# Two transformer layers with sliding-window attention on one core: priorities for evictions and masks, MLP values in half buffers, score maxima cut at PSUM banks

## The chip, the cores and the metric

One Trainium2 chip, one of its cores. The metric is the device time of one execution in microseconds. Engines are named as in the profile: PE (TensorE, its matmuls; PEld its weight loads), DVE (VectorE), ACT (ScalarE), POOL (GpSimd), SP (SyncE, which issues most transfers).

## What is computed

Two layers, each an attention block and an MLP block over 2048 tokens of width 640, with the same weights in both layers:

```python
H = 32; Dh = D // H; W = 256              # D = 640, F = 1536
qkv = (layernorm(x) @ wqkv).reshape(B, S, 3, H, Dh)
scores = einsum("bhqd,bhkd->bhqk", q, k) * Dh ** -0.5
mask = (i - j >= 0) & (i - j < W)          # i: query, j: key
p = softmax(where(mask, scores, -1e9))
x = x + einsum("bhqk,bhkd->bhqd", p, v).reshape(B, S, D) @ wo
h = layernorm(x) @ w1 + b1
x = x + (relu(h) ** 2) @ w2 + b2           # and the same again for layer 2
```

All is float32 outside. Inside, the kernel carries each operand of the projections as two float16 parts, a high one and the rest, and multiplies high by high, high by low and low by high (`mm3`, three matmuls for each step of the contraction).

## The kernel before

**Units and quads.** The tokens go in groups of T = 256. A unit `u` is one group in one layer: 8 groups by 2 layers, 16 units. The 32 heads of a unit go in 8 quads of four heads. For each quad there are three pieces of attention work:

- `max_quad`: the scores with queries on the partitions (L300, a block of 16 matmuls into the two PSUM tiles `bb` of three banks each), then on DVE, for each of four pieces (two head pairs `j`, two query blocks `i`) and two halves `e` of the partitions, an in-place add of the mask with a maximum along the row (L308, eight reduces, each followed by a read of its accumulator). A piece has 384 columns; the four lie one behind the other in the 1536 columns of a tile, so the second crosses from bank 0 to bank 1 and the third from bank 1 to bank 2. The reduces are traced after all 16 matmuls.
- `exp_quad`: the scores again, transposed, keys on the partitions, with the row maxima taken away through two extra rows of the contraction (L344, 16 matmuls into the same two `bb` tiles, one bank for each of three steps), then six exponentials on ACT (L353, each 128x512 into a tile `pt`) and the triangular masks on POOL (L362, L366, eight for a quad).
- `pv_quad`: 32 matmuls of probabilities by values into `pv` (L391), then the copy `po` out of PSUM on ACT (L401), transposes and a reciprocal on DVE (L404 to L407), the product on POOL (L408), and the split into two float16 parts `ot` (L411 on ACT, L412 on DVE). `max_out` transposes the maxima of four quads (L316), splits them into `mT` on DVE (L318, L319) and sends them into rows of `qt`.

**Dense stages.** While unit `u` does its attention, PE also does, in pieces between the quads, `stage_qk` and `stage_v` of unit `u + 1`, `stage_o` and the MLP `stage_f` of unit `u - 1`. Each accumulates in a PSUM tile `acc`, which is evicted: `qd` (L237 on ACT, then L238 on DVE), `vt` (L264 on ACT), `x1` (L442 and L491 on DVE), and in the first half of `stage_f`, for two of the 12 blocks of F at a time, two relus into one buffer `r` of 128x512 (L476, ACT), its square on POOL (L478), the high part on ACT (L479) and the rest on DVE (L480) into `hh`. The second half multiplies `hh` by w2. The tag `mm` has two PSUM buffers of one bank, shared by `acc`, `tr` and `pv`; the two `bb` tiles take the other six banks and are shared in turn by `exp_quad` and `max_quad`.

**What sets the order.** PE's order is the order in which the program traces its instructions (`manual_schedule`). `together` writes it: for each quad the exponentials' matmuls, then dense work, then the maxima's matmuls of a quad five ahead and pv, then dense work again; `SHARE` is the part of a quad's dense work that stands between the exponentials' matmuls and pv. The orders of ACT, DVE, POOL and SP are made before the run by a planner that walks through estimated times: whenever an engine is free in its plan, it takes of the instructions whose inputs are ready the one with the lowest priority number, by default the one traced first. `tc.high_priority(offset=400)` gives the instructions traced inside it a number lower by 400. On the chip an engine then keeps the order planned. Waits are put in by the framework from the tiles that the instructions read and write.

Of the kernel before, what the change touches and what calls it, by code (L numbers as in the profile page):

```python
# [42 lines left out]
def kernel(ctx: ExitStack, tc: tile.TileContext, x, wqkv, wo, w1, b1, w2, b2, out):  # L43
# [120 lines left out]
    def split_t(y, dst):  # L164

        for c0, n in ((0, 3), (3, 2)):
            tr = ps.tile([P, 4, P], F32, name="tr", tag="mm", bufs=2)
            for c in range(n):
                nc.tensor.transpose(tr[:, c, :], y[:, (c0 + c) * P:(c0 + c + 1) * P], ident)
            nc.scalar.copy(dst[:, 0, c0:c0 + n], tr[:, :n])  # L170
            nc.vector.tensor_sub(dst[:, 1, c0:c0 + n], tr[:, :n], dst[:, 0, c0:c0 + n])  # L171
            yield 117 * n

    xs = [tc.dram_tile([P, D], F32, name=f"xs{i}") for i in range(S // P)]
# [47 lines left out]
    def stage_qk(u, hold=False):  # L222
        yT = yTs[u]
        qt = sb.tile([P, NP, T], F16, name="qt", tag="qt", bufs=2)
        kt = kts[u % 3]
        qts[u] = qt
        for j, dst in enumerate((qt, kt)):
            qd = sb.tile([P, KC, 2, T], F16, name="qd", tag="qd", bufs=1)
            for c0 in range(0, KC, 2):
                n = min(2, KC - c0)  # L230
                acc = ps.tile([P, 2, T], F32, name="acc", tag="mm", bufs=2)
                for c in range(n):
                    lo = j * D + (c0 + c) * P
# [3 lines left out]
                at[0] = nc.scalar.activation(qd[:, c0:c0 + n, 0, :], acc[:, :n, :], AF.Copy, scale=s)  # L237
                nc.vector.scalar_tensor_tensor(qd[:, c0:c0 + n, 1, :], acc[:, :n, :], s, qd[:, c0:c0 + n, 0, :],  # L238
                                               op0=ALU.mult, op1=ALU.subtract)
# [16 lines left out]
    def stage_v(u):  # L256
        yT = yTs.pop(u)
        for i in range(2):
            vt = vts[(2 * u + i) % 6][0]
            for h in range(2):  # L260
                acc = ps.tile([P, 2, T], F32, name="acc", tag="mm", bufs=2).rearrange("p a n -> p (a n)")
                yield from mm3(acc[:, :HD], lambda a, k: yT[:, a, k, i * P:(i + 1) * P],
                               lambda b, k: wq_s[:, b, k, 2 * D + h * HD:2 * D + (h + 1) * HD], KC, 136)
                at[0] = nc.scalar.activation(vt[:, h * NP:(h + 1) * NP, 0:DH],  # L264
                                             acc[:, :HD].rearrange("p (h d) -> p h d", d=DH),
                                             AF.Copy, scale=1.0 / (YS * WS))


    GQ = NQ // 2
# [5 lines left out]
    def max_quad(n):  # L275

        u, qd = divmod(n, NQ)
        g = u % NG
        qt, cur, prev = qts[u], kts[u % 3], kts[(u - 1) % 3]
        G = qd // GQ  # L280
        if (u, G) not in mxs:
            mxs[u, G] = sb.tile([P, 2, 2, 2 * GQ], F32, name="mx", bufs=2)
        mx = mxs[u, G]
        bb = [b.rearrange("p a n -> p (a n)") for b in banks()]
        found = []
        for j in range(2):
            p = 2 * qd + j
            for i in range(2):
                parts = [(prev, 0, T, 0), (cur, 0, P, T)] if i == 0 else [(prev, P, T, 0), (cur, 0, T, P)]
                if g == 0:  # L290
                    parts = parts[1:]
                o = parts[0][3]
                base = 3 * P * (2 * j + i)
                for kt, a, b, c in parts:
                    while a < b:

                        z = min(b, a + 512 - (base + c) % 512)
                        for e in range(2):
                            r = slice(64 * e, 64 * e + 3 * DH)
                            nc.tensor.matmul(bb[e][:, base + c:base + c + z - a], qt[r, p, i * P:(i + 1) * P],  # L300
                                             kt[r, p, a:z], start=True, stop=True)
                        a, c = z, c + z - a
                for e in range(2):
                    s0 = p % (2 * GQ)
                    found.append((bb[e][:, base + o:base + 3 * P], maskb[:, o:], mx[:, i, e, s0:s0 + 1]))

        for w, mask, to in found:
            nc.vector.tensor_tensor_reduce(out=w, in0=w, in1=mask, scale=1.0, scalar=-3.0e38,  # L308
                                           op0=ALU.add, op1=ALU.max, accum_out=to)

    def max_out(u, G):

# [5 lines left out]
        nc.vector.tensor_scalar(mT[:, 0], tr[:NR, 0, :], -1.0 / MS, None, op0=ALU.mult)  # L318
        nc.vector.scalar_tensor_tensor(mT[:, 1], tr[:NR, 0, :], -1.0 / MS, mT[:, 0],  # L319
                                       op0=ALU.mult, op1=ALU.subtract)  # L320
        for i in range(2):
            for e in range(2):
                s0 = (2 * i + e) * 2 * GQ
# [7 lines left out]
    def exp_quad(n):  # L331
# [2 lines left out]
        qt = qts[u]  # L334
        bb = banks()
        steps = steps_of(u)
        for k, step in enumerate(steps):
            o = 0
            for kb, kt, ko, q0, qn in step:
                w = qn * P  # L340
                for j in range(2):
# [2 lines left out]
                        nc.tensor.matmul(bb[e][:, k, o:o + w], kt[r, 2 * qd + j, ko:ko + P],  # L344
                                         qt[r, 2 * qd + j, q0 * P:q0 * P + w], start=True, stop=True)
                    o += w
        out = []
        for k, step in enumerate(steps):
            pts = []
            for e in range(2):  # L350
                o = sum(2 * qn * P for _, _, _, _, qn in step)
# [3 lines left out]
                for kb, kt, ko, q0, qn in step:  # L355
                    w = qn * P
                    pj = pt[:, o2:o2 + 2 * w].rearrange("p (j n) -> p j n", j=2)
                    o2 += 2 * w
                    if kb < 2:

                        m = pj[:, :, w - P:w]
                        nc.gpsimd.affine_select(out=m, in_=m, pattern=[[0, 2], [-1, P]],  # L362
                                                compare_op=ALU.is_gt, fill=0.0, base=0, channel_multiplier=1)
                    else:
                        m = pj[:, :, 0:P]
                        nc.gpsimd.affine_select(out=m, in_=m, pattern=[[0, 2], [1, P]],  # L366
                                                compare_op=ALU.is_ge, fill=0.0, base=0, channel_multiplier=-1)
                    pts.append((e, kb, q0, qn, pj))
            out.append(pts)
        return out  # L370
# [8 lines left out]
    def pv_quad(n, quad):  # L379
# [21 lines left out]
        nc.scalar.copy(po, pv)  # L401
# [33 lines left out]
    def stage_o(u):  # L435
        for i in range(2):
            od, x1 = ols.pop((u, i))
            for h in range(2):
                acc = ps.tile([P, 2, T], F32, name="acc", tag="mm", bufs=2).rearrange("p a n -> p (a n)")
                hs = slice(h * HD, (h + 1) * HD)  # L440
                yield from mm3(acc[:, :HD], lambda a, k: od[:, k, a, :], lambda c, k: wo_s[:, c, k, hs], KC, 136)
                nc.vector.scalar_tensor_tensor(x1[:, hs], acc[:, :HD], 1.0 / (OS * WS), x1[:, hs],  # L442
                                               op0=ALU.mult, op1=ALU.add)
# [19 lines left out]
    def stage_f(u, ahead=None):  # L463
# [3 lines left out]
        hh = sb.tile([P, 2, FC, T], F16, name="hh", tag="hh", bufs=1)  # L467
        for f0 in range(0, FC, 2):
            acc = ps.tile([P, 2, T], F32, name="acc", tag="mm", bufs=2)
            r = sb.tile([P, 2, T], F32, name="r", bufs=1)  # L470
            for f in range(2):
                fo = (f0 + f) * P
                yield from mm3(acc[:, f, :], lambda a, k: w1_s[:, a, k, fo:fo + P],
                               lambda c, k: y2[:, c, k, :], KC, 109)
            for f in range(2):
                nc.scalar.activation(r[:, f, :], acc[:, f, :], AF.Relu, bias=b1s[:, f0 + f:f0 + f + 1],  # L476
                                     scale=1.0 / (YS * WS))
            nc.gpsimd.tensor_tensor(r, r, r, op=ALU.mult)  # L478
            nc.scalar.copy(hh[:, 0, f0:f0 + 2, :], r)  # L479
            nc.vector.tensor_sub(hh[:, 1, f0:f0 + 2, :], r, hh[:, 0, f0:f0 + 2, :])  # L480
        if ahead is not None:
            ln_cross(ahead)
        for i in range(2):
            b = 2 * g + i
            x1 = x1s.pop((u, i))
            for h in range(2):
# [4 lines left out]
                nc.vector.scalar_tensor_tensor(x1[:, hs], acc[:, :HD], 1.0 / WS, x1[:, hs],  # L491
                                               op0=ALU.mult, op1=ALU.add)
            dst = xs[b] if l + 1 < NL else out_rows[b * P:(b + 1) * P, :]
            nc.sync.dma_start(dst, x1)

# [6 lines left out]
        for _ in chain(*gs):  # L502
            pass

    SHARE = 0.5
    LEAD = GQ + 1
    late = []

# [139 lines left out]
```

## Time and profile before

| | |
|---|---|
| median of 3 runs | 1810.35 us (1807.04 to 1821.32) |
| the profiled execution's own time | 1810.7 us |
| its span, first to last instruction | 1809.0 us |
| mean granted TensorE clock | 0.974 |
| PE busy | 1625.9 us, 90% of the span |
| DVE busy | 1068.8 us, 59% |
| ACT busy | 765.0 us, 42% |
| POOL busy | 715.0 us, 40% |

How to read the lines that follow. A row of the waits has the engine, the tile and line of the waiting instruction, an arrow, what released it, and then the total in us, how often, and the longest. A row of the timeline has start and length in us, the engine, the line, the operation, out<-in, and the number of instructions that were merged into it; brackets at the end hold the idle time ahead of it and what ended that. A row of the table of stretches has the stretch, its length, the busy time of PE, PEld, DVE, ACT and POOL with the number of instructions, then the granted clock, the busy share of the transfer engines and the GB/s. A row of the groups has the shape, the count, the busy time in us, the mean of one in ns, and the idle time ahead with its releasers. Overlapping matmuls make a "busy" PE a little less than a full one.

### The profile page before, as it was taken

The numbers are of one execution on the slowest core, as the hardware profiler recorded it, in microseconds if no ns is written. First come the engines' busy times: TensorE is split into PE (matmuls) and PEld (weight loads), VectorE is DVE, ScalarE is ACT, GpSimd is POOL, SyncE is SP. The second block draws the span as 40 slices with busy tenths as digits, with TensorE's granted clock in tenths as the row PEclk, the third lists the DMA queues.
The fourth block names the chain that finished last, engine by engine and source line by source line (L and its number), as shares of the span: only waits on it lengthen the run. The fifth ranks groups of instructions, "written<-read, shape, count | busy, mean of one in ns | idle before, by whom it ended". The sixth has DMA issues, their size and how long they took to land.

```text
span 1809.0 us, 44389 instructions
## 1 busy us (share of the span) xinstructions
PE 1625.9 (90%) x17286; PEld 1179.0 (65%) x17286; DVE 1068.8 (59%) x3377; ACT 765.0 (42%) x1620; POOL 715.0 (40%) x1338
## 2 busy tenths in 40 slices
PE   5767698999999989999899999999999999997798
PEld 4544476676666767666677767667676666764567
DVE  6546465757666565766556666666656666655331
ACT  5464243443444344444434343444434344442422
POOL 4353343434334343433425253433525344342422
PEclk9889899999999999999999999999999999998899
DMA  6754104235151423515153422515243251511010
GB/s 198 186 162 108 42 25 120 47 89 111 35 143 42 125 56 88 111 35 143 42 134 63 121 64 77 124 34 140 45 116 66 71 129 34 139 17 56 16 37 30
DMA packets 239059, 154.81 MB, mean 86 GB/s; under 512 B 80640, under 2 KB 219776, under 8 KB 238848
## 3 DMA queue, kind: packets, MB, share of 16 engines
q1 hardware_dynamic: 230432, 142.46, 32.0%
q10 hardware_dynamic: 8416, 9.51, 1.8%
q8 instruction: 136, 2.23, 0.5%
q14 instruction: 75, 0.61, 0.1%
HBM read 82.58 MB, written 52.43 MB: 75 GB/s over the span
## 4 chain that ended last, share of the span: by engine, by line
PE 55%; DVE 20%; ACT 8%; DMA 7%; POOL 4%; issue 3%; SPq 2%; ACTq 0%; POOLq 0%; DVEq 0%
PE acc L145 42%; DVE bb L308 11%; PE pv L391 5%; ACT pt L353 5%; PE bb L300 4%; PE bb L344 4%; DVE mx L308 2%; POOL po L408 1%; DMA qk<-qd 1%; DVE bst L157 1%; SPq L326 1%; ACT r L476 1%; DMA xt<-in_A_x_dram 1%; DMA stg<-in_B_w_dram 1%; POOL pt L366 1%
## 5 line engine op out<-in xcount | busy, mean ns | idle before, releaser
L308 DVE CUSTOM_DVE_ANT_0 bb<-bb,maskb 128x384 f32<-128x384 f32 (+2 forms) x1024 | 511.2, 559 | 154.3 <-PE bb L300 154.1
L353 ACT ACTIVATE pt<-bb 128x512 f32<-128x512 f32 x736 | 368.7, 601 | 86.7 <-PE bb L344 86.4
L408 POOL TENSOR_TENSOR po<-po,rb 128x256 f32<-128x256 f32 x128 | 94.6, 739 | 675.5 <-DVE rb L407 580.4
L145 PE MATMUL acc<-y,w_s 128*128 128x256 f16 x2880 | 335.4, 275 | 3.5 <-DVE y L171 1.5
L145 PE MATMUL acc<-w_s,hh 128*128 128x320 f16 x2304 | 326.3, 299 | 0.4 <-DVE hh L480 0.2
L145 PEld LDWEIGHTS <-w_s 128*128 128x128 f16 x2880 | 278.5, 99 | 62.9 <-issue 27.5
L145 PE MATMUL acc<-yT,wq_s 128*128 128x256 f16 x2400 | 290.0, 281 | 12.0 <-DVE qd L238 7.1
L145 PEld LDWEIGHTS <-hh 128*128 128x128 f16 x2304 | 221.7, 98 | 98.4 <-issue 14.5
L145 PEld LDWEIGHTS <-wq_s 128*128 128x128 f16 x2400 | 235.5, 100 | 66.2 <-issue 33.0
L391 PE MATMUL pv<-pt,vt 128*32 128x128 f32 (+1 forms) x3840 | 202.2, 341 | 61.3 <-ACT r L476 31.8
L362 POOL TENSOR_SCALAR_AFFINE_SELECT pt<-pt 128x256 f32<-128x256 f32 x448 | 192.4, 434 | 147.5 <-ACT pt L353 134.1
L366 POOL TENSOR_SCALAR_AFFINE_SELECT pt<-pt 128x256 f32<-128x256 f32 x512 | 201.2, 416 | 9.8 <-ACT pt L353 8.9
L401 ACT COPY po<-pv 128x256 f32<-128x256 f32 x128 | 47.5, 371 | 342.7 <-PE pv L391 342.7
L391 PEld LDWEIGHTS pv<-pt,vt 128*32 128x32 f32 x3840 | 110.7, 112 | 115.6 <-issue 50.9
L145 PE MATMUL acc<-wo_s,od 128*128 128x320 f16 x960 | 143.3, 305 | 30.5 <-DMA od<-o 17.7
L145 PE MATMUL acc<-wq_s,yT 128*128 128x320 f16 x960 | 144.5, 299 | 12.8 <-DVE mT L319 7.9
L478 POOL TENSOR_TENSOR r<-r 128x512 f32<-128x512 f32 x96 | 99.9, 1041 | 116.7 <-ACT r L476 112.5
L145 PEld LDWEIGHTS <-od 128*128 128x128 f16 x960 | 92.4, 99 | 79.0 <-issue 25.4
L308 DVE DVE_READ_ACCUMULATOR2_ANT mx<- 128x1 f32 x1024 | 142.5, 139 | 0.0
L411 ACT CAST ot<-po 128x256 f16<-128x256 f32 x128 | 52.1, 407 | 195.7 <-POOL po L408 195.6
L145 PEld LDWEIGHTS <-yT 128*128 128x128 f16 x960 | 92.3, 98 | 59.6 <-issue 25.5
L238 DVE SCALAR_TENSOR_TENSOR qd<-acc,qd 128x512 f16<-128x512 f32 (+1 forms) x96 | 55.4, 578 | 126.4 <-ACT qd L237 126.4
(62 smaller groups left out, 1427.0 us busy)
## 6 DMA issues: line engine op xcount, KB each, us to landing
qk<-qd SPq DMA_DIRECT2D x32, 640.0 KB
qt<-qk SPq DMA_DIRECT2D x32, 480.0 KB
kt<-qk SPq DMA_DIRECT2D x32, 480.0 KB
qk<-qd SPq DMA_DIRECT2D x32, 320.0 KB
o<-ot SPq DMA_DIRECT2D x256, 40.0 KB
od<-o SPq DMA_DIRECT2D x32, 320.0 KB
stg<-in_B_w_dram ACTq DMA_DIRECT2D x30, 256.0 KB
xt<-in_A_x_dram SPq DMA_DIRECT2D x16, 320.0 KB
```

Source lines behind the costliest of these rows:

```text
L145: nc.tensor.matmul(acc, lhs(a, c), rhs(b, c), start=(k == 0), stop=(k == 3 * nk - 1))
L238: nc.vector.scalar_tensor_tensor(qd[:, c0:c0 + n, 1, :], acc[:, :n, :], s, qd[:, c0:c0 + n, 0, :], op0=ALU.mult, op1=ALU.subtract)
L300: nc.tensor.matmul(bb[e][:, base + c:base + c + z - a], qt[r, p, i * P:(i + 1) * P], kt[r, p, a:z], start=True, stop=True)
L308: nc.vector.tensor_tensor_reduce(out=w, in0=w, in1=mask, scale=1.0, scalar=-3.0e38, op0=ALU.add, op1=ALU.max, accum_out=to)
L344: nc.tensor.matmul(bb[e][:, k, o:o + w], kt[r, 2 * qd + j, ko:ko + P], qt[r, 2 * qd + j, q0 * P:q0 * P + w], start=True, stop=True)
L353: at[0] = nc.scalar.activation(pt[:, :o], bb[e][:, k, :o], AF.Exp, scale=SCALE / (QS * QS))
L362: nc.gpsimd.affine_select(out=m, in_=m, pattern=[[0, 2], [-1, P]], compare_op=ALU.is_gt, fill=0.0, base=0, channel_multiplier=1)
L366: nc.gpsimd.affine_select(out=m, in_=m, pattern=[[0, 2], [1, P]], compare_op=ALU.is_ge, fill=0.0, base=0, channel_multiplier=-1)
L391: nc.tensor.matmul(pv[32 * jj:32 * (jj + 1), q0 * P:(q0 + qn) * P], vf[:, c:c + 32], pj[:, j, :], start=(k == 0), stop=(k == len(steps) - ...
L408: nc.gpsimd.tensor_tensor(po, po, rb.rearrange("p a b -> p (a b)"), op=ALU.mult)
L411: nc.scalar.copy(oh, pf)
L478: nc.gpsimd.tensor_tensor(r, r, r, op=ALU.mult)
```

## The change

It has five parts.

1. A helper `first()` (priority 400 places ahead) is put around the instructions that empty the `mm` buffers in PSUM (`split_t`, `qd`, `vt`, `mT`, `po`, both `x1` updates, the relus) and around the masks on POOL.
2. In `stage_f` the buffer `r` of 128x512 becomes two buffers of 128x256, one for each block of F, and square, high part and rest are done for each by itself: 96 more of each.
3. In `max_quad` three pieces have a bank each (columns 0 to 383), and the fourth is spread over the last 128 columns of the three banks. Its matmuls come first, cut into 128 columns; its reduces come last and read three banks. The reduces of each other piece are traced behind that piece's matmuls. A quad has 18 matmuls for the maxima in place of 16 (10 in place of 8 in the first unit of a layer).
4. In `exp_quad` the exponentials and masks of a step are traced behind that step's matmuls, and no longer behind those of all three.
5. `SHARE` goes from 0.5 to 0.55.

```diff
+    def first():
+        return tc.high_priority(offset=400)
...
+                with first():
+                    at[0] = nc.scalar.activation(qd[:, c0:c0 + n, 0, :], acc[:, :n, :], AF.Copy, scale=s)
+                    nc.vector.scalar_tensor_tensor(qd[:, c0:c0 + n, 1, :], acc[:, :n, :], s, qd[:, c0:c0 + n, 0, :],
+                                                   op0=ALU.mult, op1=ALU.subtract)
...
-        bb = [b.rearrange("p a n -> p (a n)") for b in banks()]
+        bb = banks()
         found = []
-        for j in range(2):
+        for w in (3, 0, 1, 2):
+            j, i = divmod(w, 2)
             p = 2 * qd + j
...
+            if w == 3:
+                parts = [(kt, z, z + P, c + z - a) for kt, a, b, c in parts for z in range(a, b, P)]
+            for kt, a, b, c in parts:
                 for e in range(2):
+                    r = slice(64 * e, 64 * e + 3 * DH)
+                    to = bb[e][:, c // P, 3 * P:] if w == 3 else bb[e][:, w, c:c + b - a]
+                    nc.tensor.matmul(to, qt[r, p, i * P:(i + 1) * P], kt[r, p, a:b], start=True, stop=True)
+            now = []
+            for e in range(2):
...
+                if w == 3:
+                    now.append((bb[e][:, o // P:, 3 * P:], maskb[:, o:].rearrange("p (a n) -> p a n", n=P), accum))
+                else:
+                    now.append((bb[e][:, w, o:3 * P], maskb[:, o:], accum))
+            if w == 3:
+                found = now
+                continue
+            for v, mask, accum in now + (found if w == 2 else []):
+                nc.vector.tensor_tensor_reduce(out=v, in0=v, in1=mask, scale=1.0, scalar=-3.0e38,
+                                               op0=ALU.add, op1=ALU.max, accum_out=accum)
...
+        out = []
         for k, step in enumerate(steps):
...
                         nc.tensor.matmul(bb[e][:, k, o:o + w], kt[r, 2 * qd + j, ko:ko + P],
                                          qt[r, 2 * qd + j, q0 * P:q0 * P + w], start=True, stop=True)
                     o += w
-        out = []
-        for k, step in enumerate(steps):
             pts = []
...
-            r = sb.tile([P, 2, T], F32, name="r", bufs=1)
...
-            for f in range(2):
-                nc.scalar.activation(r[:, f, :], acc[:, f, :], AF.Relu, bias=b1s[:, f0 + f:f0 + f + 1],
-                                     scale=1.0 / (YS * WS))
-            nc.gpsimd.tensor_tensor(r, r, r, op=ALU.mult)
-            nc.scalar.copy(hh[:, 0, f0:f0 + 2, :], r)
-            nc.vector.tensor_sub(hh[:, 1, f0:f0 + 2, :], r, hh[:, 0, f0:f0 + 2, :])
+            rs = [sb.tile([P, T], F32, name="r", bufs=2) for f in range(2)]
+            with first():
+                for f, r in enumerate(rs):
+                    nc.scalar.activation(r, acc[:, f, :], AF.Relu, bias=b1s[:, f0 + f:f0 + f + 1],
+                                         scale=1.0 / (YS * WS))
+            for f, r in enumerate(rs):
+                nc.gpsimd.tensor_tensor(r, r, r, op=ALU.mult)
+                nc.scalar.copy(hh[:, 0, f0 + f, :], r)
+                nc.vector.tensor_sub(hh[:, 1, f0 + f, :], r, hh[:, 0, f0 + f, :])
...
-    SHARE = 0.5
+    SHARE = 0.55
```

More of the change, by code (lines that the diff above doesn't have):

```diff
@@ L317, in max_out @@
         mT = sb.tile([NR, 2, P], F16, name="mT", bufs=1)
[L318 to L320 removed]
+        with first():
+            nc.vector.tensor_scalar(mT[:, 0], tr[:NR, 0, :], -1.0 / MS, None, op0=ALU.mult)
+            nc.vector.scalar_tensor_tensor(mT[:, 1], tr[:NR, 0, :], -1.0 / MS, mT[:, 0],
+                                           op0=ALU.mult, op1=ALU.subtract)
         for i in range(2):
@@ L400, in pv_quad @@
         po = sb.tile([P, T], F32, name="po", bufs=2)
-        nc.scalar.copy(po, pv)
+        with first():
+            nc.scalar.copy(po, pv)
         rb = sb.tile([P, T // 32, 32], F32, name="rb", bufs=1)
@@ L441, in stage_o @@
                 yield from mm3(acc[:, :HD], lambda a, k: od[:, k, a, :], lambda c, k: wo_s[:, c, k, hs], KC, 136)
-                nc.vector.scalar_tensor_tensor(x1[:, hs], acc[:, :HD], 1.0 / (OS * WS), x1[:, hs],
-                                               op0=ALU.mult, op1=ALU.add)
+                with first():
+                    nc.vector.scalar_tensor_tensor(x1[:, hs], acc[:, :HD], 1.0 / (OS * WS), x1[:, hs],
+                                                   op0=ALU.mult, op1=ALU.add)
             y = sb.tile([P, D], F32, name="xt", tag="xt", bufs=2)
@@ L490, in stage_f @@
                                lambda c, k: w2_s[:, c, k, hs], FC, 136)
-                nc.vector.scalar_tensor_tensor(x1[:, hs], acc[:, :HD], 1.0 / WS, x1[:, hs],
-                                               op0=ALU.mult, op1=ALU.add)
+                with first():
+                    nc.vector.scalar_tensor_tensor(x1[:, hs], acc[:, :HD], 1.0 / WS, x1[:, hs],
+                                                   op0=ALU.mult, op1=ALU.add)
             dst = xs[b] if l + 1 < NL else out_rows[b * P:(b + 1) * P, :]
```

57 lines of the change are left out of this document (22 added, 35 removed).

## The prediction

> **What bounds the kernel now.** I read the engine shares first, then the table of stretches, the waits of PE, and the timeline of one unit (the attention of 256 tokens and the dense stages beside it).
>
> ```profile
> span 1809.0 us, 44389 instructions
> PE 1625.9 (90%) x17286; PEld 1179.0 (65%) x17286; DVE 1068.8 (59%) x3377; ACT 765.0 (42%) x1620; POOL 715.0 (40%) x1338
> ...
> 496.50:602.50 106.00, 99.41 (x1115) 72.91 (x1110) 67.55 (x209) 45.89 (x97) 42.79 (x84) 1.00 0.34 86
> ```
>
> PE is busy for 90% of the span; no other engine is near its limit. The last row is one unit: 106.00 us, PE busy 99.41, granted clock 1.00, then DVE 67.55, ACT 45.89, POOL 42.79. So a unit has 6.6 us of idle PE, and that is all that an edit of the order can win there. The waits say what it is. PE's waits in the even part, 390 to 1541 us (1151 us, or 10.9 units; total, times, longest):
>
> ```profile
> PE pv L391 <- ACT r L476: 26.6, 12, 3.1
> PE pv L391 <- POOL pt L366: 15.8, 20, 1.5
> PE acc L145 <- DVE qd L238: 13.2, 20, 1.0
> PE acc L145 <- DVE mT L319: 6.6, 10, 0.7
> PE acc L145 <- ACT vt L264: 2.3, 10, 0.3
> ...
> PE bb L344 <- DVE mx L308: 0.2, 1, 0.2
> ```
>
> The same kinds over the whole run:
>
> ```profile
> PE pv L391 <- ACT r L476: 31.8, 15, 3.1
> PE pv L391 <- POOL pt L366: 25.7, 30, 2.5
> PE acc L145 <- DVE qd L238: 19.6, 28, 2.0
> ...
> PE bb L344 <- DVE mx L308: 9.7, 14, 1.8
> PE acc L145 <- DVE mT L319: 8.5, 13, 0.7
> ```
>
> Five waits of the even part make 64.5 us. Four of them (26.6, 13.2, 6.6, 2.3) are late evictions of the two `mm` buffers in PSUM, one (15.8) is late masks. Almost nothing there waits for the maxima (0.2): their DVE work is hidden, with what margin is asked below.
>
> **The MLP values in halves.** The longest wait, once a unit:
>
> ```profile
> 565.61 1.12 ACT L353 ACTIVATE pt<-bb 128x512 f32<-128x512 f32 x2
> 566.56 0.88 ACT L476 ACTIVATE r<-acc,b1s 128x256 f32<-128x256 f32 x2
> 567.53 1.04 POOL L478 TENSOR_TENSOR r<-r 128x512 f32<-128x512 f32 x1
> 568.60 0.62 ACT L479 CAST hh<-r 128x512 f16<-128x512 f32 x1 [1.15 <-POOL r L478]
> ...
> 569.60 0.69 DVE L480 TENSOR_TENSOR hh<-r,hh 128x512 f16<-128x512 f32 x1
> 570.38 0.84 ACT L476 ACTIVATE r<-acc,b1s 128x256 f32<-128x256 f32 x2 [1.16 <-DVE hh L480]
> 571.36 1.51 PE L391 MATMUL pv<-pt,vt 128*32 128x256 f32 x32 [2.39 <-ACT r L476]
> ```
>
> One buffer `r` serves both halves, so the next relus (570.38) wait until the whole chain relu, square, cast, subtract of the pair before is through (566.56 to 570.29, 3.7 us). Their `acc` stays in PSUM and pv has no buffer for 2.39 us. With a buffer per half the chain is relu, square, cast, subtract of 256 columns. Two relus take 0.88; the others, from the groups of that shape:
>
> ```profile
> L408 POOL TENSOR_TENSOR po<-po,rb 128x256 f32<-128x256 f32 x128 | 94.6, 739 | 675.5 <-DVE rb L407 580.4 <-DVE bmv L159 92.4 <-ACT r L476 2.6
> L411 ACT CAST ot<-po 128x256 f16<-128x256 f32 x128 | 52.1, 407 | 195.7 <-POOL po L408 195.6
> L412 DVE TENSOR_TENSOR ot<-po,ot 128x256 f16<-128x256 f32 x128 | 59.2, 463 | 89.6 <-ACT ot L411 87.1
> ```
>
> A half takes 0.44 + 0.65 + 0.41 + 0.46 = 2.0 us (a half square costs between half of 1.04 and the 0.74 of another POOL operation of that shape; I take 0.65). Started at 566.56, the first relu of the next pair is free at about 568.7, the second at 569.3, its eviction is done at 569.8, and pv, ready at 568.97, waits 0.85; relus ahead of the second exponential of 565.61 start 0.4 earlier. I leave 0.55 a unit, 6.0 in all: **-20.6** of 26.6 (bounds 0 and 26.6). The halves add one cast, one square and one subtract 96 times: 2 x 407 - 625 = 0.19 us of ACT, up to 0.44 of POOL, 0.17 of DVE, six times a unit: 1.1, 2.6 and 1.0 us beside 60, 63 and 38 us of idle time. They are hidden by PE's 99 us; without that cover they would cost the sum, 4.7 a unit.
>
> **Masks first, exponentials bank by bank, SHARE.** The wait for POOL in the quad before:
>
> ```profile
> 549.48 0.83 PE L344 MATMUL bb<-qt,kt 62*128 62x256 f16 x16
> 551.20 0.41 ACT L411 CAST ot<-po 128x256 f16<-128x256 f32 x1 [1.33 <-POOL po L408]
> 551.51 3.03 ACT L353 ACTIVATE pt<-bb 128x512 f32<-128x512 f32 x6
> 552.53 1.06 POOL L478 TENSOR_TENSOR r<-r 128x512 f32<-128x512 f32 x1
> ...
> 556.90 1.51 PE L391 MATMUL pv<-pt,vt 128*32 128x256 f32 x32 [1.36 <-POOL pt L366]
> ```
>
> The exponentials start 1.20 us after their matmuls are through (549.48 + 0.83), since a cast that waits for POOL stands ahead of them; a handover takes about 0.1 (relus end at 567.44, the square starts at 567.53), so they are 1.1 late. The masks then stand behind a square of 1.06 us. Three edits bear on this. Masks ahead of the square give up to 1.06. Tracing each step's exponentials behind its own matmuls lets the first start after 4 of the 16 matmuls, at most 0.5 us earlier. SHARE 0.55 moves 0.05 of the dense work of a quad (72 us of matmul pace a unit, 9 a quad, an estimate from 99.4 less the blocks of 0.83, 0.83 and 1.51) from behind pv to ahead of it: 0.45. The cast ahead of the exponentials stays. I take two thirds: **-10.5** of 15.8 (bounds 0 and 15.8).
>
> **Evictions first.** The wait for `qd`, and that for `mT`:
>
> ```profile
> 507.15 0.64 DVE L238 SCALAR_TENSOR_TENSOR qd<-acc,qd 128x512 f16<-128x512 f32 x1
> 507.84 1.25 PE L145 MATMUL acc<-yT,wq_s 128*128 128x256 f16 x10 [0.41 <-DVE qd L238]
> ...
> 536.75 0.68 DVE L162 TENSOR_SCALAR xt<-x,bmv 128x640 f32<-128x640 f32 x1 [0.91 <-POOL bmv L161]
> 537.35 0.27 DVE L319 SCALAR_TENSOR_TENSOR mT<-tr,mT 32x128 f16<-32x128 f32 x1
> 537.68 2.20 PE L145 MATMUL acc<-wq_s,yT 128*128 128x320 f16 x15 [0.66 <-DVE mT L319]
> ```
>
> The `qd` subtract (507.15) stands behind the last reduces of its quad, which follow each other at about 0.5; one place ahead it ends 0.5 earlier, more than the 0.41 that PE waits. I take four fifths: **-10.6**. The second half of `mT` stands behind a normalization that itself waits 0.91; its 0.27 fits into these 0.91, the buffer is free 0.7 us or more before 537.62, and PE doesn't wait: **-6.6**. The 2.3 on `vt` are left. What the moved evictions issue behind them (the `qd` writes on SP's queue, the weight loads tied to `at[0]` on ACT's queue at the start) keeps its order or comes earlier; the squares, the normalization and the b2 addition on POOL now stand behind masks of 0.41, and nobody on PE waits for them within a quad.
>
> **What is late next: the maxima.** They are pushed back by what goes ahead, and the next exponentials need their banks. Two margins, the first in the quad of the `r` chain:
>
> ```profile
> 561.78 0.14 DVE L308 DVE_READ_ACCUMULATOR2_ANT mx<- 128x1 f32 x1
> ...
> 562.82 0.83 PE L344 MATMUL bb<-qt,kt 62*128 62x256 f16 x16
> ...
> 600.66 0.14 DVE L308 DVE_READ_ACCUMULATOR2_ANT mx<- 128x1 f32 x1
> ...
> 601.96 0.83 PE L344 MATMUL bb<-qt,kt 62*128 62x256 f16 x16
> ```
>
> 0.90 us from the last reduce to the matmul that needs the bank, and 1.16 in a quad near the unit's end. Read in the same way, four of the eight quads of this unit have 0.9 to 1.2, the others 1.8 to 3.9. SHARE takes 0.45 of each; the removed pv wait of 1.36 sits just ahead of this one. Against that, reduces by bank can start before all 16 matmuls are through, by about 0.3 us. 0.90 - 1.36 - 0.45 + 0.27 = -0.64: a new wait of 0.64 a unit, **+7.0** (bounds 0 and the +40 of a rival below).
>
> **Pieces by banks.** The fourth piece is cut into three matmuls of 128 columns, 256 more matmuls in all.
>
> ```profile
> L300 PE MATMUL bb<-kt,qt 60*128 60x256 f16 x960 | 105.6, 276 | 6.6 <-ACT pt L353 6.4
> ...
> L300 PE MATMUL bb<-kt,qt 60*128 60x128 f16 x960 | 71.8, 220 | 1.0 <-DVE mx L308 0.8 <-DMA kt<-qk 0.2
> ```
>
> 128 columns more make a matmul 56 ns longer, which is their whole streaming time: a block of 0.83 has four pairs of each width, 4 x 110 + 4 x 55 plus a tail of 0.17. Two of 128 then cost what one of 256 did: **0**. If pairs cost the same whatever their width, it would be 82 ns a quad, +9; columns decide, as the 56 shows. A reduce over three banks is taken at its old time; 0.1 us on two of eight would be 0.2 of a margin.
>
> **The sum.** Even part: -20.6 - 10.5 - 10.6 - 6.6 + 7.0 = -41.3. Outside of it the same four kinds leave 31.8 + 25.7 + 19.6 + 8.5 - 62.2 = 23.4; at the same share (48.3 of 62.2) -18.2; the waits of exponentials for maxima there (9.5, 13 times) grow by 0.45 each, +5.9. The sum, -12.3, is halved, as transfers pace the start: -6. Together -47.3. The profiled execution took 1810.7 us for its span of 1809.0, 0.35 above the median shown, so no correction is needed: 1810.7 - 47.3 = **1763**.
>
> **The rivals.**
> *The wait moves to the maxima.* The four tight quads (0.9 to 1.2) lose 0.45 to SHARE and 1.24 to two evictions of about 0.62 put ahead, 0.6 under zero each: 4 x 0.6 x 16 units = 40, of which 7 are counted: 1763 + 33 = 1796. For it: DVE is PE's first companion, with 67.55 busy in a unit. Against: most evictions already run between the reduces.
> *The order hardly changes.* The order is fixed before the run from estimated times; where an eviction and a reduce are not ready together there, priority does nothing. Then only halves and SHARE act: -20.6 - 4 (the same wait outside) - 20 x 0.45 + 7 = -27: 1784. Against: in the `qd` and `mT` rows both were ready.
> *Slower: a late eviction at the head of the queue.* An engine runs its order as fixed, so a relu put ahead of exponentials whose matmuls come late holds them all. The cast at 551.20 shows the price: exponentials 1.1 late, PE 1.36. From 35 quads of 128 on (47.3/1.36) the gain is gone; in half of them it costs 87: 1850. For it: the priority is large, 400 places, more than a quad. Against: evictions mostly become ready when PE stands right behind them.
> The Trainium skill, "TensorE: Matmul & The Clock Gate", section "Architectural detail" (engine queue depths), speaks for this one: ACT and DVE are strict FIFOs, nothing overtakes. The trace agrees (exponentials ready at 550.3, started at 551.51). By that rule alone each early eviction is a possible stall; how many are, it can't say.
> *The readers hold PE.* If a step's matmuls had to wait for the reads of the step before though those are in another bank, each quad would hold PE for some five reads of 0.6: far above 2000. Against: in the diff no matmul writes a bank that an earlier step's or piece's read still uses; the fourth piece, which touches all three, is written first and read last.
> The Trainium skill, "PSUM — Partial Sum Buffer", section "PSUM bank collisions raise a hardware error", orders two engines only where bank and quadrant are the same; no row here has one tile read and written at once, so no run shows it yet.
>
> **How the numbers follow.** Forecast 0.60, order hardly changed 0.12 (both faster by over 1%, about what a measurement tells from no change), wait moved to the maxima 0.15 (within 1%), head of the queue 0.11 and readers 0.02 (slower). So faster 0.72, same 0.15, slower 0.13. The likeliest alone: 1740 to 1785 (its terms at their bounds). The range: below, all 64.5 of the even part and half of the 23.4 outside, 1810.7 - 64.5 - 11.7 = 1734; above, the rival at the head of the queue at 42 quads, 1763 + 57 = 1820.
>
> **What would show it.** Right: pv's wait for `r` under 10 us, for masks under 10; `qd` and `mT` gone from PE's list; bb L344 waiting for `mx` up by 5 to 15; a unit at 101 to 103 us; 17542 matmuls at the same busy time. Wrong: exponentials starting over 1.2 us behind the end of their matmuls in most quads, new PE waits of over 2 us a unit on `mx` or `pt`, or a maxima block longer than 0.9 us.

## The result, and the profile after

The changed kernel takes 2665.62 us (median of 4 runs, 2660.45 to 2683.83), the kernel before 1811.84 beside it (1807.04 to 1821.32): a ratio of 1.472, 95% interval 1.463 to 1.481. The forecast was 1763, the range ended at 1820. What came is the rival with a chance of 0.02, "the readers hold PE".

The page of the kernel after: span, busy times, the granted clock in 40 slices.

```profile
span 2665.0 us, 45823 instructions
PE 2097.6 (79%) x17542; PEld 1343.8 (50%) x17542; DVE 1124.1 (42%) x3473; ACT 810.4 (30%) x1716; POOL 728.6 (27%) x1434
...
PEclk9888888888888888888998888888888888888789
```

The span is 856 us longer. PE's idle time went from 183 us (1809.0 - 1625.9) to 567 (2665.0 - 2097.6), +384; its busy time rose by 472, though only 256 short matmuls were added. The clock's row, mostly 8, belongs to a mean of 0.851, against 0.974 before. The idle time has an address. PE's waits, kernel after:

```profile
PE bb L308 <- DVE mx L321: 270.0, 486, 4.3
PE bb L359 <- ACT pt L366: 241.4, 455, 3.3
...
PE acc L149 <- DVE qd L244: 2.7, 3, 2.0
...
PE pv L405 <- ACT r L493: 0.7, 2, 0.5
```

Two new kinds, 511 us in 941 waits, 0.54 us each: the matmuls of the maxima wait for reduces, those of the exponentials for exponentials. The waits that the change aimed at (`qd`, `r`) are nearly gone, since PE now arrives everywhere late. One maxima block of the kernel after in the timeline:

```profile
903.73 0.51 PE L308 MATMUL bb<-kt,qt 60*128 60x128 f16 x10
...
904.63 0.55 DVE L321 CUSTOM_DVE_ANT_0 bb<-bb,maskb 128x384 f32<-128x384 f32 x1
905.09 0.14 DVE L321 DVE_READ_ACCUMULATOR2_ANT mx<- 128x1 f32 x1
905.09 0.60 DVE L321 CUSTOM_DVE_ANT_0 bb<-bb,maskb 128x384 f32<-128x384 f32 x1
905.29 0.21 PE L308 MATMUL bb<-kt,qt 60*128 60x128 f16 x1 [1.04 <-DVE mx L321]
...
905.61 0.14 DVE L321 DVE_READ_ACCUMULATOR2_ANT mx<- 128x1 f32 x1
905.80 0.32 PE L308 MATMUL bb<-kt,qt 60*128 60x128 f16 x3 [0.30 <-DVE mx L321]
```

After 10 matmuls (the fourth piece and piece 0) PE stops. The next matmul writes bank 1, and goes 0.06 us after the accumulator of the reduce in bank 0 is read (905.09 + 0.14): half `e` = 0. The next stop ends with the accumulator of half `e` = 1 (905.61 + 0.14). The two tiles `bb` are told apart, the three banks inside one are not.

The same tile-wide wait, the other way round, stood in the kernel before (timeline):

```profile
501.78 0.83 PE L300 MATMUL bb<-kt,qt 60*128 60x256 f16 x16
...
502.65 0.57 DVE L308 CUSTOM_DVE_ANT_0 bb<-bb,maskb 128x384 f32<-128x384 f32 x1 [1.08 <-PE bb L300]
```

The first reduce reads columns that the first few of these matmuls wrote, and starts 0.04 us after the last of the 16 (502.61). There it cost nothing.

The busy time: the groups of PE by line, kernel before and then kernel after (busy us, mean ns).

```profile
L145 PE MATMUL acc<-w_s,hh 128*128 128x320 f16 x2304 | 326.3, 299 | 0.4 <-DVE hh L480 0.2
L391 PE MATMUL pv<-pt,vt 128*32 128x128 f32 (+1 forms) x3840 | 202.2, 341 | 61.3 <-ACT r L476 31.8 <-POOL pt L366 25.7 <-DVE qd L238 3.0
L300 PE MATMUL bb<-kt,qt 60*128 60x128 f16 (+1 forms) x1920 | 107.2, 248 | 7.6 <-ACT pt L353 6.4 <-DVE mx L308 0.8 <-DMA kt<-qk 0.2
```

```profile
L149 PE MATMUL acc<-w_s,hh 128*128 128x320 f16 x2304 | 372.4, 326 | 0.0
L405 PE MATMUL pv<-pt,vt 128*32 128x128 f32 (+1 forms) x3840 | 293.9, 473 | 1.7 <-DVE qd L244 1.0 <-ACT r L493 0.7
L308 PE MATMUL bb<-kt,qt 60*128 60x128 f16 (+1 forms) x2176 | 216.1, 245 | 272.9 <-DVE mx L321 270.0 <-DVE bmv L163 1.1 <-DMA kt<-qk 0.4
```

The dense group is the same work, unbroken, and takes 1.141 times as long; the mean clocks stand as 0.974/0.851 = 1.145. pv, which comes straight behind the broken maxima, takes 1.45 times as long, and there the clock is far below its mean. The stretch of the pv block behind the maxima shown above:

```profile
907.70:910.50 2.80, 2.80 (x34) 1.44 (x34) 2.17 (x8) 0.00 (x0) 0.00 (x0) 0.50 0.00 0
```

At 0.50 the 32 matmuls of pv take 2.79 us, where they took 1.51 before. So the clock has to be counted where PE is busy: laid over PE's busy time, the clock records of the two traces give a mean of 0.825 after and 0.977 before, and 368 us lost to the clock against 37. That is 331 of the 472 us. What is left, 141 over 941 breaks, is 0.15 us a break, and it goes with the blocks that are cut: the maxima's double (107.2 to 216.1 us). One matmul by itself takes 0.21 us in the lines above, three take 0.32, ten 0.51, and a block of 16 before took 0.83. This split is worked out, not measured by itself.

### The profile page after: what moved, and what is told of

Same layout as the page of the kernel before. It is cut to its first block, busy times and chain, and to the rows that moved or that the text cites. A ratio compares the mean times of both kernels' runs of the same rounds, so it can differ in the third digit from the quotient of the medians.

```text
span 2665.0 us, 45823 instructions
## 1 busy us (share of the span) xinstructions
PE 2097.6 (79%) x17542; PEld 1343.8 (50%) x17542; DVE 1124.1 (42%) x3473; ACT 810.4 (30%) x1716; POOL 728.6 (27%) x1434
## 4 chain that ended last, share of the span: by engine, by line
PE 61%; ACT 11%; DVE 10%; issue 9%; DMA 5%; SPq 3%; POOL 2%; ACTq 0%; DVEq 0%; POOLq 0%
PE acc L149 41%; PE pv L405 10%; ACT pt L366 7%; PE bb L359 5%; PE bb L308 4%; DVE bb L321 3%; SPq L340 2%; DVE mx L321 2%; DMA xt<-xs 1%; DMA stg<-in_B_w_dram 1%; ACT hh L497 1%; ACT r L493 1%; DVE bst L161 1%; ACT yl L214 1%; DMA stg<-in_A_wo_dram 1%
## 5 line engine op out<-in xcount | busy, mean ns | idle before, releaser
L366 ACT ACTIVATE pt<-bb 128x512 f32<-128x512 f32 x736 | 392.9, 586 | 206.5 <-PE bb L359 204.2
L308 PE MATMUL bb<-kt,qt 60*128 60x128 f16 (+1 forms) x2176 | 216.1, 245 | 272.9 <-DVE mx L321 270.0
L359 PE MATMUL bb<-qt,kt 62*128 62x128 f16 (+1 forms) x1920 | 212.8, 258 | 245.3 <-ACT pt L366 241.4
L149 PE MATMUL acc<-y,w_s 128*128 128x256 f16 x2880 | 388.2, 302 | 1.5 <-DVE y L176 1.5
L149 PE MATMUL acc<-w_s,hh 128*128 128x320 f16 x2304 | 372.4, 326 | 0.0
L405 PE MATMUL pv<-pt,vt 128*32 128x128 f32 (+1 forms) x3840 | 293.9, 473 | 1.7 <-DVE qd L244 1.0
L308 PEld LDWEIGHTS <-qt 60*128 60x128 f16 x2176 | 95.3, 95 | 381.1 <-issue 378.8
L359 PEld LDWEIGHTS <-kt 62*128 62x128 f16 x1920 | 87.0, 94 | 357.5 <-issue 351.5
L498 DVE TENSOR_TENSOR hh<-r,hh 128x256 f16<-128x256 f32 x192 | 84.7, 458 | 259.9 <-ACT hh L497 253.1
L405 PEld LDWEIGHTS pv<-pt,vt 128*32 128x32 f32 x3840 | 149.1, 150 | 82.8 <-issue 67.2
L496 POOL TENSOR_TENSOR r<-r 128x256 f32<-128x256 f32 x192 | 117.8, 634 | 156.2 <-ACT r L493 155.9
```

What stands on the lines that cost most here:

```text
L149: nc.tensor.matmul(acc, lhs(a, c), rhs(b, c), start=(k == 0), stop=(k == 3 * nk - 1))
L308: nc.tensor.matmul(to, qt[r, p, i * P:(i + 1) * P], kt[r, p, a:b], start=True, stop=True)
L366: at[0] = nc.scalar.activation(pt[:, :o], bb[e][:, k, :o], AF.Exp, scale=SCALE / (QS * QS))
L405: nc.tensor.matmul(pv[32 * jj:32 * (jj + 1), q0 * P:(q0 + qn) * P], vf[:, c:c + 32], pj[:, j, :], start=(k == 0), stop=(k == len(steps) - ...
L498: nc.vector.tensor_sub(hh[:, 1, f0 + f, :], r, hh[:, 0, f0 + f, :])
```

## The experiments

Theory: the framework orders a matmul behind every read of its PSUM tile traced ahead of it, whatever the bank; that alone makes the loss. Rival A: the chip itself can't write one bank while another is read. Rival B: the added matmuls, or reduces over three banks. Ratios are to the kernel before, run beside.

**The reads traced last again**, all other parts of the change kept:

```diff
-            for v, mask, accum in now + (found if w == 2 else []):
+            found = found + now if w == 3 else found[:-2] + now + found[-2:]
+        for v, mask, accum in found:
...
+        out = []
+        for k, step in enumerate(steps):
```

> The changed kernel with the reads of a quad's PSUM tiles (reduces, exponentials) traced behind all of its matmuls again; priorities, half buffers, layout by banks and SHARE 0.55 stay. Theory T (a matmul waits for every read of its tile that was traced ahead of it, whatever the bank): both waits, 270 us on the maxima and 241 us on the exponentials, go to under 20 us, the granted clock is back above 0.95, the time near 1763 us (1735 to 1800). Theory P (evictions and masks put ahead starve the maxima and exponentials, and PE waits for those): the waits stay, over 2300 us.

1812.12 us, 0.998 (0.996 to 1.000). The whole loss is gone: PE busy 1627.0 with 17542 matmuls, clock 0.977. So the order of tracing made it, not the matmuls. But none of the forecast gain appeared either, and the time is above the range expected. The waits, kernel with the reads last:

```profile
PE acc L149 <- DVE qd L244: 26.6, 29, 1.9
PE bb L356 <- DVE mx L319: 20.7, 30, 2.8
...
PE bb L356 <- DVE rc L420: 12.6, 16, 1.1
PE pv L404 <- ACT r L492: 9.9, 13, 2.0
PE pv L404 <- POOL pt L379: 9.0, 10, 2.5
...
PE acc L149 <- ACT r L492: 6.0, 11, 0.6
PE pv L404 <- POOL pt L375: 5.4, 10, 1.4
```

Against the rows of before in the prediction: pv lost 21.9 us of waiting for `r` and 11.9 for masks (whose two lines had 25.7 and 0.6), and PE got 11.0 more on `mx`, 7.0 on `qd`, and 11.2 and 5.3 on `rc` and on `acc` for `r`, which had 1.4 and 0.7 before: -33.8 and +34.5.

**Each early read alone**, put into the kernel before: the exponentials by step, and the maxima by pieces (as in the change, parts 4 and 3).

```diff
+        out = []
         for k, step in enumerate(steps):
...
-        out = []
-        for k, step in enumerate(steps):
```

> The kernel before with one edit: the exponentials and masks of a step are traced behind that step's matmuls. Theory T: PE waits for exponentials in front of steps 2 and 3 as in the changed kernel, some 240 us in all; of the 854 us lost the share 241/511 is 400 us, so near 2215 us (2080 to 2300), with a clock near 0.9. Theory P: no priorities here, so 1800 to 1830 us.

> The kernel before with one edit: the maxima's pieces by banks, the fourth over three, each piece's reduces traced behind its matmuls. Theory T: PE waits for reduces in front of pieces 2 and 3, some 270 us; the share 270/511 of 854 us is 450 us, near 2260 us (2120 to 2350). Theory P: 1800 to 1830 us.

2202.36 us, 1.213 (1.209 to 1.218), and 2193.44, 1.209 (1.204 to 1.213): +388 and +379 us, together 767 of the 854. Both lie in the ranges of theory T. The first one adds no matmul and no strided reduce, so rival B falls. PE's longest wait in the one and in the other:

```profile
PE bb L345 <- ACT pt L352: 244.4, 463, 3.5
```

```profile
PE bb L301 <- DVE mx L314: 254.3, 479, 2.6
```

**A tile for each bank**, with the early reads and all other parts kept. The fourth piece gets its own bank, and its matmuls are traced behind pv, where a bank is free:

```diff
-        return [ps.tile([P, 3, 512], F32, name="bb", tag="bb", bufs=2) for e in range(2)]
+        return ps.tile([P, 512], F32, name="bk", tag="bk", bufs=6)
...
-                max_quad(m)
+                rest_of = max_quad(m)
...
+            if rest_of is not None:
+                rest_of()
```

> The changed kernel with a PSUM tile of its own for each bank (six of 512 columns in place of two of 1536), reads traced behind each step's or piece's matmuls as in the changed kernel; the fourth piece has a tile of its own and stands behind pv, uncut. Theory T (the wait is put in when the program is made, by tile): no such waits, exponentials start about 0.45 us after the first matmul of their quad, near 1755 us (1725 to 1800). Rival H (the chip holds PE while another engine reads the neighbouring banks): the waits stay though the tiles are separate, above 2300 us.

1802.03 us, 0.993 (0.991 to 0.995), 2 us above the range expected. The reads are traced as early as in the kernel after, and of the 511 us of holds 24.0 are left: 21.7 and 1.8 us in which the maxima's matmuls wait on `mx` and `pt`, 0.5 in which the exponentials' matmuls wait on `mx`. One block of the exponentials in this kernel's timeline:

```profile
305.64 0.83 PE L352 MATMUL bk<-qt,kt 62*128 62x256 f16 x16
306.13 3.05 ACT L359 ACTIVATE pt<-bk 128x512 f32<-128x512 f32 x6 [0.77 <-PE bk L352]
```

ACT begins to read the banks of the first step 0.49 us after the first matmul, and PE writes on into the others for 0.34 us without a stop: the 16 take 0.83 us, as before. Rival A falls: the chip lets PE write one bank while another is read, and the hold is a wait that the program carries. That agrees with the section cited in the prediction (the Trainium skill, "PSUM — Partial Sum Buffer", "PSUM bank collisions raise a hardware error"): order is needed only within one bank and quadrant. The framework asks for more.

**Dense work of about 1.5 us between steps and between pieces** of the kernel after, so that PE has something to do while the reads run:

```diff
+            if w < 2:
+                fill()
...
+            if k + 1 < len(steps):
+                fill()
```

> The changed kernel with dense matmuls (about 1.5 us) traced between the steps of the exponentials and between the pieces of the maxima, so that PE has other work where its next step has to wait. Theory T with the clock (the loss is idle PE, the clock that falls with it, and nothing else): the waits on pt and mx fall from 511 us to under 150, the granted clock is above 0.95, 1820 to 1950 us. Rival (each wait costs by itself, through its semaphore and the drained pipeline, some 0.9 us for each of 941): above 2300 us.

1997.76 us, 1.105 (1.097 to 1.113), above what I had expected: the idle time and its clock are not all of the loss. Waits, kernel with the dense work between:

```profile
PE bb L308 <- DVE mx L321: 44.0, 77, 2.2
PE bb L361 <- DVE mx L321: 39.8, 67, 1.5
PE bb L361 <- ACT pt L368: 30.6, 61, 1.3
...
PE bb L308 <- ACT pt L368: 11.3, 20, 2.0
```

511 us of holds are down to 126 and the clock is back at 0.956, so the clock followed the breaks. Idle PE is 228 us, 45 above before; busy PE 1777.3, 151 above, of which the clock, counted as above, makes 34. The other 118, about the size of the 141 above, go with blocks cut small; this run doesn't part them further.

**The parts of the gain alone**, each in the kernel before: the priorities, the half buffers (part 2 of the change without its `first()`), SHARE.

```diff
+        return tc.high_priority(offset=400)
```

> The kernel before with the priorities alone (evictions out of PSUM and masks 400 places ahead). With reads traced last the rest of the change came to 1812 us, not 1763: something gives back what the rest wins. Theory A (SHARE 0.55 takes the time that the maxima need in front of the next exponentials, and that gives the gain back): priorities win here, qd and mT leave PE's list, 1785 to 1800. Theory B (an eviction put ahead pushes the maxima and exponentials back, so the priorities themselves lose what they win): qd waits go down, waits on mx go up by as much, 1805 to 1825.

```diff
+            rs = [sb.tile([P, T], F32, name="r", bufs=2) for f in range(2)]
```

> The kernel before with the MLP values in two half buffers alone. Both theories: pv's wait for the relus goes from 31.8 to under 12 us. By the forecast's term that is 20 to 25 us: 1785 to 1792. If the freed time comes back as another wait, 1803 to 1815.

```diff
-    SHARE = 0.5
+    SHARE = 0.55
```

> The kernel before with SHARE 0.55 alone. Theory A: pv's wait for masks shrinks by some 9 us, the exponentials' wait for maxima grows by 20 or more, 1815 to 1830. Theory B: 1798 to 1812.

Priorities 1814.22 us, 0.999 (0.996 to 1.002); halves 1808.39, 0.998 (0.996 to 1.000); SHARE 1817.55, 1.003 (1.001 to 1.005). The time with the priorities fits theory B and that with SHARE theory A, but neither mechanism is there: the priorities don't shorten the wait for `qd`, and SHARE lengthens that for `mx` by 4.9 us, not 20. With the priorities, 21 of DVE's 3377 instructions change their place in the order that the trace shows, 14 of ACT's 1620 and 2 of POOL's 1338, and the waits are those of before: 31.8 on `r`, 25.8 on masks, 19.4 on `qd`, 7.9 on `mT`. To see whether 400 places were too few:

```diff
-        return tc.high_priority(offset=400)
+        return tc.high_priority(offset=4000)
```

> The priorities alone with 4000 places in place of 400. With 400 the order of DVE's 3380 instructions kept 3360 in place, ACT's 1643 of 1661. If the planner seldom has an eviction and a reduce ready together, 4000 places change as little: the same waits, 1805 to 1822. If 400 places were too few, qd and mT go down by over 10 us together.

A single run: 1812.78 us, and DVE, ACT and POOL in the order of the run with 400. So the size is not it. By the planner's rule it follows that in the plan an eviction and a reduce are seldom ready at the same moment; the plan itself is not on record.

Why the halves gain little, in the quad of the `r` chain: the six exponentials ahead of it in the kernel before, then the timeline of the kernel with the halves.

```profile
563.68 3.04 ACT L353 ACTIVATE pt<-bb 128x512 f32<-128x512 f32 x6
```

```profile
564.99 0.41 ACT L411 CAST ot<-po 128x256 f16<-128x256 f32 x1 [2.37 <-POOL po L408]
...
565.30 3.03 ACT L353 ACTIVATE pt<-bb 128x512 f32<-128x512 f32 x6
...
568.18 0.88 ACT L476 ACTIVATE r<-acc,b1s 128x256 f32<-128x256 f32 x2
...
570.71 0.47 ACT L476 ACTIVATE r<-acc,b1s 128x256 f32<-128x256 f32 x1
...
571.56 0.47 ACT L476 ACTIVATE r<-acc,b1s 128x256 f32<-128x256 f32 x1 [0.37 <-DVE hh L481]
...
572.18 1.51 PE L391 MATMUL pv<-pt,vt 128*32 128x256 f32 x32 [1.59 <-ACT r L476]
```

From the first relu of one pair to that of the next it is 2.53 us (before: 3.82; worked out: 2.1). But the second relu follows only at 571.56, and the eviction is done 3.85 us after the first relu of the pair before, where 3.24 were worked out and 4.66 measured before. That is the 0.8 us by which pv's wait falls, from 2.39 to 1.59. The quad is late besides. In both kernels the first pair stands behind all six exponentials, and these now start 1.62 us later, since the cast `ot` ahead of them waits for the product on POOL until 564.99 (before: 563.29). The first pair comes 1.62 us later with them, and `acc` waits 0.55 us for it, which it didn't before.

**A tile for each bank, taken apart.** Tiles alone in the kernel before; with the halves at SHARE 0.5; with all parts at SHARE 0.6.

> The kernel before with a PSUM tile for each bank alone: exponentials and reduces start behind their own matmuls, the fourth piece stands behind pv; no priorities, one buffer r, SHARE 0.5. The waits for masks (25.7 us) should fall by 0.45 us each 30 times, 13 us; the maxima's last piece starts 1.5 us later but its reduces have to wait for the others anyway. 1790 to 1805; if it is no better than before, the 0.993 of the version with all parts comes from the parts together.

> Tiles of their own for each bank and the half buffers, without priorities, SHARE 0.5. Own tiles alone were 1832, all parts with SHARE 0.55 1802. If the half buffers make the difference, 1800 to 1812 here; if SHARE 0.55 does, 1822 to 1832.

> All parts with a tile for each bank, SHARE 0.6 in place of 0.55. With own tiles the maxima start earlier than before, so that less time behind pv is enough: 1790 to 1803 if masks and relus still bound (pv's waits 10.4 and 8.8 us go down); 1805 to 1825 if the maxima now come late.

1832.09 us, 1.011 (1.007 to 1.015); 1805.57, 0.998 (0.997 to 1.000); 1785.95, 0.988 (0.985 to 0.991). Tiles alone miss the range: pv's waits for masks didn't fall (26.9 us in two lines), that for `r` rose from 31.8 to 40.8, and PE was busy 17.6 us longer; why is open. The half buffers on these tiles make 26.5 us, where in the kernel before they made 3.4. The last version is below its range and beats both kernels. Three more runs take its parts away: its priorities; its tiles and its priorities; and SHARE one step further.

> One PSUM tile per bank, half buffers and SHARE 0.6, without the priorities; otherwise as the version measured at 1785.95 us. Theory 1, priorities move next to nothing in the planned order, so the gain there came from tiles, halves and SHARE together: 1781 to 1791, ratio 0.983 to 0.991, with the waits of pv on r under 5 us as there. Rival, priorities matter once each bank is free by itself (evictions and reduces are then ready together more often): 1797 to 1807, ratio 0.993 to 0.998, and pv waits for r or for masks by 10 us or more again.

> The kernel before with half buffers and SHARE 0.6, its two PSUM tiles of three banks, no priorities. Theory 1, with three banks in one tile the time taken from pv's waits comes back as waits of the exponentials' matmuls on the maxima (14.6 us at 0.55): 1804 to 1816, ratio 0.996 to 1.002, bb on mx 20 us or more. Rival, the dense work ahead of pv is what pays and tiles don't matter: 1780 to 1795, ratio 0.982 to 0.990.

> As the version measured at 1785.95 us, with SHARE 0.65. Theory 1, the fourth piece and the reduces now come later still and the next exponentials' matmuls wait for them: 1785 to 1800, ratio 0.986 to 0.994, waits on mx above 30 us (23.4 at 0.6). Rival, the gain of 16 us from 0.55 to 0.6 goes on: 1765 to 1780, ratio 0.975 to 0.984.

Without priorities 1783.15 us, 0.986 (0.981 to 0.991): they have no part in the gain. Without the tiles too 1818.34, 1.005 (1.003 to 1.007), a little above what was expected: the tiles are what lets SHARE pay. (With the tiles come the early reads and the fourth piece's place behind pv; no run parts the three.) At 0.65 1799.5, 0.995 (0.992 to 0.997). The waits with halves and SHARE 0.6, first on the old tiles, then on a tile for each bank (no priorities in either):

```profile
PE bb L344 <- DVE mx L308: 20.3, 30, 2.6
PE bb L344 <- DVE rc L406: 18.4, 20, 2.2
...
PE bb L300 <- ACT pt L353: 11.2, 20, 1.7
PE pv L391 <- ACT r L476: 10.9, 17, 2.5
PE pv L391 <- POOL pt L366: 8.8, 11, 2.0
```

```profile
PE bk L298 <- DVE mx L303: 23.6, 31, 1.2
...
PE pv L389 <- POOL pt L364: 9.8, 13, 1.6
...
PE pv L389 <- ACT r L474: 2.9, 6, 1.0
```

On both, pv's waits are small. On the old tiles the scores' matmuls pay 49.9 us for it, on a tile for each bank 23.6 and two kinds of 1.9 and 1.1. At SHARE 0.65 the waits on `mx` fall to 11.1, not rise as expected; 13.2 on `r` and 17.1 on a load of `y` come up instead (1.6 and 4.8 at 0.6).

## Why the prediction was wrong

**The rival that came.** The step that failed is the sentence "in the diff no matmul writes a bank that an earlier step's or piece's read still uses". True, and beside the point: the wait goes by tile. The price was right in kind (some reads per quad, "far above 2000"), the chance of 0.02 was not. The prediction even used the tile-wide rule in one direction, counting as a gain that exponentials need no longer wait for all 16 matmuls, and didn't ask what the same rule does to matmuls traced behind those exponentials. The fence from 501.78 us shows where it could be read.

**What the rival lacked** was the second half of its price: 384 us are idle PE, 472 are PE busy for longer, 331 of them by the clock.

**Evictions first, -10.6 and -6.6.** Measured alone, 19.6 to 19.4 and 8.5 to 7.9 over the whole run: nothing. The argument "in the `qd` and `mT` rows both were ready" took readiness on the chip for readiness in the plan. The rival "the order hardly changes" was right in its mechanism, though not in its 1784 (1812 with the reads last), and "a late eviction at the head of the queue" had no ground, since little was moved.

**Halves, -20.6.** The chain was sized too short: in the quad shown the eviction is done 3.85 us behind the first relu, not 3.24, so 0.8 us of 2.39 are won and not 1.84. pv's wait for `r` fell from 31.8 to 23.7 over the run and that for masks from 25.7 to 20.6, but the wait of `acc` for `r` rose from 0.7 to 6.1 and that on `mx` from 9.7 to 14.6: 3.4 us are left in the time. "Relus ahead of the second exponential" didn't come either: with the reads last, which has the priorities, they stand behind all six too. That the exponentials, and the relus with them, would start later was not in the sum.

**Masks, exponentials by step, SHARE, -10.5.** (The 72 us of matmul pace in it come out as 74 by its own terms; the 0.45 stays.) Tracing the exponentials by step was one half of the loss (+388 us alone). SHARE alone took 2.6 us from pv's wait for the masks of L366 and 12.0 from that for `r`, and gave 1.4 to the masks of L362, 4.9 to `mx`, 7.4 to `qd` and 6.7 to `acc` for `r`.

**The new wait on the maxima, +7.0** (and 5.9 outside). With the reads last it grew by 11.0 over the run under its own name, and by 11.2 booked under `rc`, a DVE instruction that touches no `bb` and stands behind the reduces in DVE's order; that both are one wait is my reading. With it the rival "the wait moves to the maxima" describes that run best: pv's gain, spent on the scores' matmuls.

**Pieces by banks, 0.** Right: 256 more matmuls left PE's busy time at 1627.0 against 1625.9 with the reads last. A block of 18 in that kernel's timeline:

```profile
551.32 0.84 PE L308 MATMUL bb<-kt,qt 60*128 60x128 f16 x18
```

0.84 us, where 16 took 0.83.

## What to carry to other kernels

Before a read is moved up between matmuls, ask by what unit the waits of the program go: two banks in one tile are one thing to it, and the profile before shows the unit where a reader of the first columns starts only after the last write. Give what shall overlap its own tile, and only then shift work: here tiles alone were 1.1% slower, the shift with the halves 0.5% slower, and all three 1.4% faster. A priority moves an instruction only where the plan has it ready beside another; look at the order it gives before counting on it.

## What the runs showed of the hardware

Many short waits of PE lower its granted clock, though they are 0.54 us in the mean and 4.3 at the longest. The table of stretches of 3 us, kernel after, behind an exponentials block broken by waits of 0.74, 0.27 and 1.38 us:

```profile
911.00:914.00 3.00, 3.00 (x25) 2.17 (x23) 2.08 (x6) 0.95 (x2) 0.73 (x1) 1.00 0.00 0
914.00:917.00 3.00, 1.61 (x18) 0.80 (x16) 2.00 (x5) 1.88 (x5) 1.53 (x3) 1.00 0.39 77
917.00:920.00 3.00, 1.88 (x9) 0.79 (x9) 1.36 (x3) 2.46 (x5) 0.00 (x0) 0.55 0.85 169
920.00:923.00 3.00, 3.00 (x13) 1.73 (x12) 0.03 (x1) 0.50 (x2) 2.30 (x2) 0.50 0.46 86
923.00:926.00 3.00, 3.00 (x20) 1.98 (x19) 0.00 (x0) 0.44 (x1) 2.89 (x7) 0.81 0.04 11
```

The clock (third number from the end) falls to 0.55 at the end of 6 us in which PE was busy for 3.5, and is at 0.50 while PE is fully busy again: 13 matmuls in 3 us, then 20, where there were 25. A longer stretch of the kernel after:

```profile
865.00:1020.00 155.00, 123.31 (x1004) 77.07 (x1007) 66.00 (x199) 44.13 (x93) 39.65 (x81) 0.81 0.20 49
```

PE is busy for 80% of it, at a mean clock of 0.81. The clock records of these traces hold two values alone, 1.00 and 0.50: the kernel after has 201 stretches at 0.50, 174 of them 3.41 us long, the kernel before 19. Over the runs the mean clock goes down as the holds grow: 0.974 before, 0.956 with 126 us of them, 0.91 with about 250 (each early read alone), 0.851 with 511.

The Trainium skill, "TensorE: Matmul & The Clock Gate", section "A second HAM failure mode: psum-queue depth-cycling", describes this for another kernel: short idle moments of PE between groups of matmuls make the clock swing, and the cost is that of slowing and warming again. The trace agrees, with 941 waits of 0.54 us in the mean, and with the clock back at 0.956 when 126 of 511 us are left.
